# A long convolution and its soft mixture of experts on one core: first stage in three products, second-stage transfers in pairs, z loads in two blocks

One core of one Trainium2 chip. The metric is the device time of one execution in microseconds (us), the median of several runs. A ratio always compares fast runs of the same rounds on the same chip.

## The reference

```python
# x (8, 5696, 128), h (5696, 128); all float32
Xf = np.fft.rfft(x, n=2*S, axis=1); Hf = np.fft.rfft(h, n=2*S, axis=0)
y  = np.fft.irfft(Xf * Hf[None], n=2*S, axis=1)[:, :S, :]     # causal long convolution
x  = y.reshape(B * S, D)                                      # 45568 tokens
logits = x @ phi                                              # 8 experts x 4 slots
d = softmax over tokens;  slot_input = d.T @ x
slot_out[e] = max(slot_input[e] @ w1[e], 0) @ w2[e]
out = softmax over slots (logits) @ slot_out
```

## The kernel before

The transform of length 90 x 64 is done with matrix products, in three stages that a loop of steps runs side by side. A step `t` takes four columns and the four mirrored ones of one group (`h`, then the eight batches; eight steps a group).

- **First stage** (`stage_a`): load a piece of x, form sums and differences of mirrored columns on GpSimd (`fold`), two 128x128 products for the sums and two for the differences, evict on ScalarE, write to the array `f` in HBM.
- **Second stage** (`stage_b1`, `stage_b2`): for each unit (two frequencies; 23 a group, three a step) load `g` from `f`, product, multiply by the transform of h on VectorE, product back, evict, write to `z` in HBM.
- **Third stage** (`stage_c1` and on): once for two steps (a pair), load 90 rows of `z`, products, then logits and the running softmax.

All transfers of the loop are issued by SyncE, in program order.

```python
# first stage, once for the sums (comp 0), once for the differences (comp 1)
for G in range(2):
    p = bank()
    nc.tensor.matmul(p[:, :], s1[:, tab[G], :], src, start=True, stop=True)        # L204
    nc.scalar.activation(st[:, :, G, :], p, AF.Copy)                               # L206
for a, p in enumerate((F0, F1)):                       # two writes of 45 rows, 1 KB runs
    nc.sync.dma_start(out=fd[g][a, n0:n0 + CH] ..., in_=st[p:p + NP] ...)          # L210
# ... cut ...
t_ = bpool.tile([P, 2, 2, D], F32, name="gt", tag="gt", bufs=5)   # one unit, 256 KB
nc.sync.dma_start(out=t_ ..., in_=fd[g] ...)                                       # L223
# ... cut: in the loop, AHEAD = 4 ...
u = us.pop(0); prefetch(u + AHEAD); stage_b1(u)        # g is asked for four units ahead
# ... cut ...
st = bpool.tile([P, 2, 2 * D], F32, name="zst", tag="zst", bufs=3)
nc.scalar.activation(st, bz, AF.Copy); nc.sync.dma_start(out=zd[g - 1] ..., in_=st)  # L281, L282
# ... cut ...
zring = [ypool.tile([P, 2, CH, 2, D], F32, name=f"zc{i}") for i in range(2)]
# load_z: 90 rows of 8 KB to partitions 20..109; two of them a pair                  # L307
```

The tile framework adds the waits.

Of the kernel before, what the change touches and what calls it, by code (L numbers as in the profile page):

```python
# [10 lines left out]
F32 = mybir.dt.float32  # L11
# [5 lines left out]

def transform_tables(S, N1, N2, CH, Z0, X0, F0, F1):












    N, R1, HALF, P = N1 * N2, S // N2, N2 // 2, 2 * N2
    k1 = np.arange(N1)
    alpha = np.pi * (k1 + 0.5) / N1
    m1 = np.arange(R1) - (N1 - 1) / 2
    a1 = np.outer(m1, alpha)
    s1 = np.stack([np.cos(a1), -np.sin(a1), -np.cos(a1)], 1)
    a0 = np.outer(alpha, np.arange(N1 // 2) + 0.5)
    i1 = np.stack([np.cos(a0), -np.sin(a0), -np.cos(a0)], 1)
    NP = N1 // 2
    part = s1  # L40
    s1 = np.zeros((P, 3, P))
    for a, p in enumerate((F0, F1)):
        s1[X0:X0 + R1, :, p:p + NP] = part[:, :, a * NP:(a + 1) * NP]
    i1 = np.pad(i1[np.arange(N1).reshape(2, N1 // 2).T.reshape(-1)],
                [(Z0, P - N1 - Z0), (0, 0), (0, N2 - N1 // 2)])
    k2 = np.arange(N2)
    omega = np.pi * (k1[:, None] + 2 * N1 * k2[None] + 0.5) / N
    m2 = np.arange(HALF) - (N2 - 1) / 2
    a2 = m2[None, :, None] * omega[:, None, :]
    w = np.concatenate([np.cos(a2), np.sin(a2)], 1)  # L50
    back = np.arange(N2).reshape(2, HALF // CH, CH).transpose(1, 0, 2).reshape(-1)
    NU = (NP + 1) // 2
    turn = (N1 - 1) / 2 * alpha[:, None] + (N2 - 1) / 2 * omega
    wq = np.zeros((2, N2, NP, N2))
    vq = np.zeros((2, N2, NU, 2, N2))
    tn = np.zeros((2, N2, 2, NU, 2))
    for a in range(2):
        wq[a] = w[a * NP:(a + 1) * NP].transpose(1, 0, 2)
        for q in range(NP):
            vq[q % 2, :, q // 2, a] = w[a * NP + q][back].T  # L60
            tn[q % 2, :, 0, q // 2, a] = np.cos(turn[a * NP + q]) / N
            tn[q % 2, :, 1, q // 2, a] = np.sin(turn[a * NP + q]) / N
    wq, vq, tn = [t.reshape(P, *t.shape[2:]) for t in (wq, vq, tn)]
    return [np.ascontiguousarray(t, dtype=np.float32) for t in (s1, i1, wq, vq, tn)]
# [3 lines left out]
def kernel(  # L68
# [42 lines left out]
    SPLIT = R1 // 16 * 16  # L111
    Z0, X0, F0, F1 = 20, 20, 6, 82
    ctx.enter_context(tc.manual_schedule())

    t_s1, t_i1, t_w, t_v, t_turn = [
        nc.inline_tensor(t, f"tab_{n}").ap()
        for n, t in zip(("s1", "i1", "w", "v", "turn"), transform_tables(S, N1, N2, CH, Z0, X0, F0, F1))]
    fd = [nc.dram_tensor(f"f_{g}", (2, N2, NP, 2, D), F32, kind="Internal").ap() for g in range(B + 1)]
# [33 lines left out]

    s1 = apool.tile([P, 3, P], F32, name="s1", tag="s1", bufs=1)
    wt = fconst.tile([P, NP, HP], F32, name="wt")
# [10 lines left out]
    xs = {}  # L165
    xf = [apool.tile([P, CH, D], F32, name=f"x{i}", tag=f"x{i}", bufs=1) for i in range(2)]
    xcs = [apool.tile([P, 2, CH, D], F32, name=f"xc{i}", tag=f"xc{i}", bufs=1) for i in range(3)]
# [20 lines left out]
    def fold(c, comp):  # L188
        if c not in xs:
            return  # L190
        t_ = xs.pop(c) if comp else xs[c]
        y_ = xf[comp]
        nc.gpsimd.tensor_tensor(out=y_[:, :, :], in0=t_[:, 0, :, :], in1=t_[:, 1, ::-1, :],  # L193
                                op=AL.subtract if comp else AL.add)
        folded[(c, comp)] = y_

    def stage_a(c, comp):
        g, j = divmod(c, NJ)
        src = folded.pop((c, comp))
        tab = (0, 1) if comp == 0 else (1, 2)  # L200
        st = apool.tile([P, CH, 2, D], F32, name="fst", tag="fst", bufs=3)
        for G in range(2):
            p = bank()
            nc.tensor.matmul(p[:, :], s1[:, tab[G], :],  # L204
                             src[:, :, :].rearrange("p n d -> p (n d)"), start=True, stop=True)
            nc.scalar.activation(st[:, :, G, :],  # L206
                                 p[:, :].rearrange("p (n d) -> p n d", d=D), AF.Copy)
        n0 = comp * HALF + CH * j
        for a, p in enumerate((F0, F1)):
            nc.sync.dma_start(  # L210
                out=fd[g][a, n0:n0 + CH, :, :, :].rearrange("n q c d -> q n (c d)"),
                in_=st[p:p + NP, :, :, :].rearrange("k n c d -> k n (c d)"))


    gs, prods = {}, {}

    def load_g(u):
        if u >= (B + 1) * NU:
            return
        g, i = divmod(u, NU)  # L220
        n = min(2, NP - 2 * i)
        t_ = bpool.tile([P, 2, 2, D], F32, name="gt", tag="gt", bufs=5)
        nc.sync.dma_start(  # L223
            out=t_[:, 0:n, :, :].rearrange("p q c d -> p (q c d)"),
            in_=fd[g].rearrange("a r q c d -> (a r) (q c d)")[:, 4 * i * D:(4 * i + 2 * n) * D])
        gs[u] = t_

# [39 lines left out]
    def stage_b2(u):  # L267
# [6 lines left out]
        for q in range(n):  # L274
            r = slice(q * HP, (q + 1) * HP)
            for a in range(2):
                nc.tensor.matmul(bz[a * HP:(a + 1) * HP, q, 0:2 * D], vt[r, i, a, :],  # L277
                                 y_[r, a, :, :].rearrange("p c d -> p (c d)"),
                                 start=True, stop=True)
        st = bpool.tile([P, 2, 2 * D], F32, name="zst", tag="zst", bufs=3)  # L280
        nc.scalar.activation(st[:, 0:n, :], bz[:, 0:n, 0:2 * D], AF.Copy)  # L281
        nc.sync.dma_start(  # L282
            out=zd[g - 1][2 * i:2 * i + n, :, :, :].rearrange("q r c d -> r q (c d)"),
            in_=st[:, 0:n, :])

# [3 lines left out]
    ybufs = [ypool.tile([P, Q * CH, D + 1], F32, name=f"y{i}") for i in range(2)]  # L289
    zring = [ypool.tile([P, 2, CH, 2, D], F32, name=f"zc{i}") for i in range(2)]  # L290
    lt = ypool.tile([P, CH, 2, HP], F32, name="lt")
    dt = ypool.tile([P, CH, 2, HP], F32, name="dt")
    om, op = [ypool.tile([P, CH, D], F32, name=n) for n in ("om", "op")]
    yt = ypool.tile([D, Q * CH, 2, MH], F32, name="yt")
    for t_ in zring:
        nc.vector.memset(t_[:, :, :, :, :], 0.0)
    for t_ in (lt, dt):
# [3 lines left out]

    def load_z(c):
        b, j = divmod(c, NJ)
        t_ = zring.pop(0)
        zring.append(t_)
        w_ = 2 * CH * 2 * D
        nc.sync.dma_start(  # L307
            out=t_[Z0:Z0 + N1, :, :, :, :].rearrange("k o n c d -> k (o n c d)"),
            in_=zd[b].rearrange("q (a r) c d -> (q a) (r c d)",
                                a=2)[:, j * w_:(j + 1) * w_])  # L310
        zs[c] = t_

    def load_pair(T):
        if T < NT:
            load_z(2 * T)
            load_z(2 * T + 1)

    def stage_c1(T, between):
        za, zb = zs.pop(2 * T), zs.pop(2 * T + 1)
        y_ = ybufs[T % 2]  # L320
# [5 lines left out]
        def product(o, tab, q):  # L326
            p = bank()
            for h_, t_ in enumerate((za, zb)):
                nc.tensor.matmul(p[h_ * HP:(h_ + 1) * HP, :], i1[:, tab, :], t_[:, o, :, q, :],  # L329
                                 start=True, stop=True)  # L330
            return p[:, :].rearrange("p (n d) -> p n d", d=D)
# [197 lines left out]
    last_front = queue[-1][1] + 1  # L529
    AHEAD = 4  # L530
    loaded = 0

    load_x(0)
    nc.scalar.dma_start(out=s1[:, :, :], in_=t_s1)
    for c in range(1, 3):
# [9 lines left out]
    for t in range(steps):  # L545
# [6 lines left out]
        def prefetch(last):  # L552
            nonlocal loaded
            while loaded < len(queue) and queue[loaded][0] <= last \
                    and queue[loaded][0] // NU * NJ + NJ <= t:
                load_g(queue[loaded][0])
                loaded += 1

        def slot_b():
            fresh = bool(us)  # L560
            if fresh:
                u = us.pop(0)
                prefetch(u + AHEAD)
                stage_b1(u)
                wait_b2.append(u)
# [11 lines left out]
        if t < NA:  # L577
            load_x(t + 3)
            stage_a(t, 0)
            fold(t + 1, 0)  # L580
        if pair(3) is not None:
            dispatch(pair(3))
# [17 lines left out]
        if t < NA:  # L600
            stage_a(t, 1)
            fold(t + 1, 1)
        if pair(1) is not None:
# [8 lines left out]
        if t == NJ:  # L612
            prefetch(AHEAD)
        if t == NA:
# [5 lines left out]
        if t == last_front:  # L620
# [6 lines left out]
            w2s = last.tile([P, E, NFC, D], F32, name="w2s")  # L627
            for i in range(2):
                t_ = last.tile([P, 2, CH, 2, D], F32, name=f"zd{i}")
                nc.vector.memset(t_[:, :, :, :, :], 0.0)  # L630
                zring.insert(i, t_)
            assert pair(1) is not None
# [12 lines left out]
        if 0 <= i < E // 2:  # L645
            nc.sync.dma_start(
                out=w2s[:, 2 * i:2 * i + 2, :, :],
                in_=moe_w2[2 * i:2 * i + 2].rearrange("e (p c) d -> p e c d", p=P))
    assert list(Ls) == [NT - 1] and not (ys or ds or prods or gs or zs or xs or folded or wait_b2
                or kept or landed)  # L650
# [131 lines left out]
```

## Time and profile before

| | kernel before |
|---|---|
| median of 4 runs | 988.72 us (983.49 to 992.83) |
| profiled span | 980.8 us |
| steps 27 to 71 (all three stages at work) | 11.75 us each, alternately 10.64 and 12.87 |
| transfers issued a step | 13.2 |

"Step" times come from the starts of the first-stage products in the timeline. In a chain of waits each share is time in which the end of the program hung on that line; "X <- Y" in a wait table means that X stood still until Y.

### The profile page before, as it was taken

The numbers are of one execution on the slowest core, as the hardware profiler recorded it, in microseconds if no ns is written. First come the engines' busy times: TensorE is split into PE (matmuls) and PEld (weight loads), VectorE is DVE, ScalarE is ACT, GpSimd is POOL, SyncE is SP. The second block draws the span as 40 slices with busy tenths as digits, with TensorE's granted clock in tenths as the row PEclk, the third lists the DMA queues.
The fourth block names the chain that finished last, engine by engine and source line by source line (L and its number), as shares of the span: only waits on it lengthen the run. The fifth ranks groups of instructions, "written<-read, shape, count | busy, mean of one in ns | idle before, by whom it ended". The sixth has DMA issues, their size and how long they took to land.

```text
span 980.8 us, 20314 instructions
## 1 busy us (share of the span) xinstructions
PE 862.6 (88%) x7220; PEld 403.2 (41%) x7220; DVE 671.7 (68%) x1137; ACT 510.8 (52%) x1051; POOL 462.4 (47%) x427
## 2 busy tenths in 40 slices
PE   6778788899999999999999999999998887875893
PEld 2222233334444444444444444444443333332883
DVE  2034577568888878777878787777788996554542
ACT  3557545445666655556555565555554443443442
POOL 5546532245555555555555555555533432694000
PEclk9979999999999999999999999999999997797875
DMA  7988899899999998998999899989998996853598
GB/s 193 269 260 266 266 324 327 270 312 295 301 294 313 296 299 276 287 303 261 307 289 297 266 298 287 300 261 288 306 279 264 297 285 190 247 174 122 224 406 328
DMA packets 177283, 272.79 MB, mean 278 GB/s; under 512 B 15024, under 2 KB 119728, under 8 KB 171423
## 3 DMA queue, kind: packets, MB, share of 16 engines
q1 hardware_dynamic: 176607, 271.13, 88.7%
q8 instruction: 58, 0.95, 0.4%
q10 hardware_dynamic: 576, 0.36, 0.2%
q14 instruction: 42, 0.34, 0.1%
HBM read 143.04 MB, written 128.39 MB: 277 GB/s over the span
## 4 chain that ended last, share of the span: by engine, by line
PE 55%; DMA 22%; POOL 7%; DVE 6%; issue 3%; ACT 3%; SPq 2%; DVEq 0%; ACTq 0%; POOLq 0%
PE bank L204 19%; PE bank L329 11%; PE bt L237 9%; DMA z<-zst 8%; PE bz L277 6%; DMA zc<-z 5%; POOL y L348 5%; DMA out_dram<-o 4%; DMA gt<-f 3%; PE bank L357 3%; PE bank L442 2%; PE bank L366 2%; PE bank L395 1%; DVE yf L263 1%; DMA f<-fst 1%
## 5 line engine op out<-in xcount | busy, mean ns | idle before, releaser
L204 PE MATMUL bank<-x,s 128*128 128x512 f32 x576 | 287.3, 626 | 9.5 <-POOL x L193 7.9
L193 POOL TENSOR_TENSOR x<-xc 128x512 f32<-128x512 f32 x144 | 183.4, 1275 | 141.0 <-PE bank L204 124.6
L281 ACT ACTIVATE zst<-bz 128x512 f32<-128x512 f32 (+1 forms) x184 | 108.3, 588 | 222.6 <-PE bz L277 138.5
L206 ACT ACTIVATE fst<-bank 128x512 f32<-128x512 f32 x288 | 168.6, 597 | 86.0 <-PE bank L204 69.0
L258 DVE TENSOR_TENSOR pr<-bt,Hr 128x512 f32<-128x512 f32 (+1 forms) x184 | 126.6, 688 | 81.3 <-PE bt L237 77.2
L237 PE MATMUL bt<-gt,wt 64*64 64x256 f32 x1620 | 138.2, 404 | 37.6 <-PE bz L277 9.9
L263 DVE TENSOR_TENSOR yf<-pr,pi 128x512 f32<-128x512 f32 (+1 forms) x184 | 158.1, 859 | 6.4
L204 PEld LDWEIGHTS bank<-x,s 128*128 128x128 f32 x576 | 100.5, 193 | 132.8 <-issue 89.0
L329 PE MATMUL bank<-zc,i 128*64 128x512 f32 x480 | 137.6, 620 | 17.3 <-ACT y L338 11.4
L261 DVE TENSOR_TENSOR pi<-bt,Hi 128x512 f32<-128x512 f32 (+1 forms) x184 | 125.2, 681 | 0.0
L277 PE MATMUL bz<-yf,vt 64*64 64x256 f32 x1440 | 118.1, 382 | 7.0 <-DVE yf L263 4.5
L237 PEld LDWEIGHTS bt<-gt,wt 64*64 64x64 f32 x1620 | 44.4, 132 | 154.7 <-PE bank L204 52.4
L348 POOL TENSOR_TENSOR y<-y,op 128x512 f32<-128x512 f32 x64 | 75.7, 1183 | 59.2 <-DVE op L334 56.6
L348 POOL TENSOR_TENSOR y<-y,om 128x512 f32<-128x512 f32 x64 | 85.4, 1334 | 2.5
L403 POOL MEMSET dt<- 64x8 f32 x32 | 3.4, 107 | 175.8 <-ACT dn L406 115.3
L277 PEld LDWEIGHTS bz<-yf,vt 64*64 64x64 f32 x1440 | 53.4, 132 | 45.0 <-issue 9.5
L357 PE MATMUL bank<-ident,y 109*128 109x109 f32 x512 | 60.7, 266 | 10.5 <-POOL y L348 10.4
L329 PEld LDWEIGHTS bank<-zc,i 128*64 128x64 f32 x480 | 32.5, 138 | 87.3 <-issue 40.5
L359 ACT ACTIVATE yt<-bank 128x360 f32<-128x360 f32 x128 | 53.0, 471 | 29.3 <-PE bank L357 29.2
L248 DVE SCALAR_TENSOR_TENSOR Hr<-bt,turn,ph 128x128 f32<-128x128 f32 (+1 forms) x46 | 16.0, 349 | 76.0 <-ACT ph L246 76.0
L357 PEld LDWEIGHTS bank<-ident,y 109*128 109x128 f32 x512 | 49.6, 143 | 26.4 <-POOL y L348 17.0
L334 DVE TENSOR_TENSOR y<-bank,y 128x512 f32<-128x512 f32 x32 | 22.1, 690 | 44.9 <-ACT y L338 36.8
(95 smaller groups left out, 911.1 us busy)
## 6 DMA issues: line engine op xcount, KB each, us to landing
f<-fst SPq DMA_DIRECT2D x288, 180.0 KB
gt<-f SPq DMA_DIRECT2D x198, 256.0 KB
z<-zst SPq DMA_DIRECT2D x176, 256.0 KB
zc<-z SPq DMA_DIRECT2D x60, 720.0 KB
xc<-in_x_dram SPq DMA_DIRECT2D x64, 320.0 KB
out_dram<-o SPq DMA_DIRECT2D x16, 1024.0 KB
out_dram<-o SPq DMA_DIRECT2D x8, 768.0 KB
c_t<-cst SPq DMA_DIRECT2D x26, 180.0 KB
```

The source lines that it names most:

```text
L193: nc.gpsimd.tensor_tensor(out=y_[:, :, :], in0=t_[:, 0, :, :], in1=t_[:, 1, ::-1, :], op=AL.subtract if comp else AL.add)
L204: nc.tensor.matmul(p[:, :], s1[:, tab[G], :], src[:, :, :].rearrange("p n d -> p (n d)"), start=True, stop=True)
L206: nc.scalar.activation(st[:, :, G, :], p[:, :].rearrange("p (n d) -> p n d", d=D), AF.Copy)
L237: nc.tensor.matmul(bt[q * HP:(q + 1) * HP, a, 0:2 * D], wt[r, 2 * i + q, :], t_[r, q, :, :].rearrange("p c d -> p (c d)"), start=True, sto ...
L258: nc.vector.tensor_tensor(out=pr[r, :, :, :], in0=pv, in1=Hr[r, i, :, :].unsqueeze(2).broadcast_to([n * HP, 2, 2, D]), op=AL.mult)
L261: nc.vector.tensor_tensor(out=pi[r, :, :, :], in0=pv, in1=Hi[r, i, :, :, :], op=AL.mult)
L263: nc.vector.tensor_tensor(out=y_[r, :, :, :], in0=pr[r, :, :, :], in1=pi[r, :, ::-1, :], op=AL.add)
L277: nc.tensor.matmul(bz[a * HP:(a + 1) * HP, q, 0:2 * D], vt[r, i, a, :], y_[r, a, :, :].rearrange("p c d -> p (c d)"), start=True, stop=True)
L281: nc.scalar.activation(st[:, 0:n, :], bz[:, 0:n, 0:2 * D], AF.Copy)
L329: nc.tensor.matmul(p[h_ * HP:(h_ + 1) * HP, :], i1[:, tab, :], t_[:, o, :, q, :], start=True, stop=True)
L348: nc.gpsimd.tensor_tensor(out=part_, in0=part(v, 0), in1=o_[:, :, :], op=sign)
L357: nc.tensor.transpose(p[:, i * TR:(i + 1) * TR], ys[T][0:TR, k * CH + i, 0:D], ident[0:TR, 0:TR])
```

## The change

The intent: (1) the four first-stage products have 90 useful columns of 128; side by side in column halves the same work fits into three. (2) Fewer, longer transfers in the second stage. (3) z loads of 16 KB runs, in a block of 64 rows and one of 26, so that the engines meet the ports of the on-chip memory evenly.

```diff
-        for G in range(2):
-            nc.tensor.matmul(p[:, :], s1[:, tab[G], :], src ...)
+        n = 1 if late else 2                     # two products early in the step, one late
+        for G in range(n):
+            for h_ in range(2):                  # sums in columns 0..63, differences in 64..127
+                nc.tensor.matmul(p[h_ * HP:(h_ + 1) * HP, :], s1[:, h_, 2 * late + G, :],
+                                 folded[(c, h_)] ...)
-        for a, p in enumerate((F0, F1)):         # 2 writes, twice a step
+        # early: for each half 45 + 15 rows in 1 KB runs; late: 60 rows in 512 B runs: 6 writes a step
-        t_ = bpool.tile([P, 2, 2, D], F32, name="gt", tag="gt", bufs=5)
+        t_ = bpool.tile([P, 4, 2, D], F32, name="gt", tag="gt", bufs=2)      # two units, 512 KB
-                prefetch(u + AHEAD)
+                prefetch(u + 2 - u % NU % 2)
-        st = bpool.tile([P, 2, 2 * D], F32, name="zst", tag="zst", bufs=3)
+        if i % 2 == 0:
+            zst.append(bpool.tile([P, 4, 2 * D], F32, name="zst", tag="zst", bufs=2))
+        # ... evict into its half; one write for two units
-    zring = [ypool.tile([P, 2, CH, 2, D], F32, name=f"zc{i}") for i in range(2)]
+    zring = [ypool.tile([P, 2, 2, CH, 2, D], F32, name="zc")]
+        for r, n, p in [(0, 64, 32), (64, 26, 0)]:    # rows, count, first partition; 16 KB runs
+            nc.sync.dma_start(out=t_[p:p + n] ..., in_=zd[b] ...[r:r + n, ...])
     # cut: both folds of the next step at once, into a second pair of tiles; tables; a zero-filled tile
```

## The prediction

> **What bounds the kernel now.** I read the page first (busy shares, the slices, the chain), then the windows by stage, then the groups with shapes, the timeline of one step, and last the records of the single DMA packets.
>
> ```profile
> PE 862.6 (88%) x7220; PEld 403.2 (41%) x7220; DVE 671.7 (68%) x1137; ACT 510.8 (52%) x1051; POOL 462.4 (47%) x427
> ...
> PE 55%; DMA 22%; POOL 7%; DVE 6%; issue 3%; ACT 3%; SPq 2%; DVEq 0%; ACTq 0%; POOLq 0%
> PE bank L204 19%; PE bank L329 11%; PE bt L237 9%; DMA z<-zst 8%; PE bz L277 6%; DMA zc<-z 5%; POOL y L348 5%; DMA out_dram<-o 4%; DMA gt<-f 3%; PE bank L357 3%; PE bank L442 2%; PE bank L366 2%; PE bank L395 1%; DVE yf L263 1%; DMA f<-fst 1%
> ```
>
> TensorE carries 55% of the chain and its largest piece is the first stage (L204, 19%); but the chain keeps crossing over to transfers of the intermediate arrays (z 8 and 5%, gt 3%). The windows (columns: stretch, length, busy us of each engine with counts, granted clock, mean share of the 16 DMA engines, GB/s) say why:
>
> ```profile
> 140.00:300.00 160.00, 149.24 (x1174) 63.95 (x1172) 119.99 (x188) 86.06 (x161) 72.79 (x62) 0.99 0.97 303
> 300.00:500.00 200.00, 194.58 (x1603) 86.22 (x1600) 159.41 (x256) 113.83 (x224) 106.28 (x92) 1.00 0.96 289
> ...
> 930.00:981.00 51.00, 32.68 (x431) 29.69 (x427) 19.29 (x32) 16.30 (x32) 0.00 (x0) 0.60 0.95 366
> ```
>
> From 140 to 700 us both TensorE (97%) and the DMA engines (96%) are full. And the DMA engines are full at 289 GB/s, while the output stage gets 366 out of the same share: there the bytes are cheap, here they are dear. The packet records give the medians 46 ns for 1 KB, 84 for 2 KB, 159 for 4 KB (a line: 8.5 ns + 37.6 per KB), but 511 for the 8 KB packets of the z loads, where the line and their own minimum say 309. One pair's z load (180 packets) takes 6.3 to 6.8 us even when little else moves.
>
> A step is one pass of the main loop. By the starts of the first-stage products in the timeline, steps 0 to 8 take 3.5 to 4.2 us, 10 to 17 about 7.6, 18 to 24 8.3, and the 44 steps from 202.5 to 719.6 us 11.75 on average: every second one a steady 10.65 (TensorE without a gap), the other 11.2 to 14.4, in which the z loads and z writes are waited for. The best pairs take 21.6 us, the average 23.5; so TensorE alone would give some 10.8 a step, and waits on transfers add the rest.
>
> ```profile
> L204 PE MATMUL bank<-x,s 128*128 128x512 f32 x576 | 287.3, 626 | 9.5 <-POOL x L193 7.9 <-ACT fst L206 1.5
> L206 ACT ACTIVATE fst<-bank 128x512 f32<-128x512 f32 x288 | 168.6, 597 | 86.0 <-PE bank L204 69.0 <-DMA f<-fst 14.4 <-DMA z<-zst 1.5
> L281 ACT ACTIVATE zst<-bz 128x512 f32<-128x512 f32 x176 | 105.2, 598 | 219.8 <-PE bz L277 135.9 <-DMA z<-zst 72.9 <-PE bank L329 6.4
> ```
>
> To be seen here: a product instruction lists 626 ns, its eviction 597; the first stage hardly waits for its own operands (9.5 us); and ScalarE waited 72.9 us for a z staging buffer to be written out, the plainest sign in the profile that writes fall behind.
>
> **What the Trainium skill says.** "TensorEngine Tiling (Array Packing)", Theoretical Speedup: column tiles of at most 64 outputs give up to 2x. The trace agrees for the third stage, which already works so: eight 128x64 instructions of 512 columns take 1.87 to 1.93 us (L329), as long as four 128x128 ones (L204, 1.91 to 1.98). "DMA: Bandwidth & Descriptors", Why a DMA increments its semaphore by 16: the transfer uses the largest count up to 16 that divides the slowest dimension on both sides. So 45 and 90 rows run on 15 engines, 64 rows on 16, 26 on 13. No view of the kernel before shows single engines, so this is taken on trust. "SBUF — State Buffer", Door 1: a transfer's partitions decide which of 16 ports it uses. 64 rows from partition 32 cover all 16, 4 rows each; 90 rows from 20, six to an engine, collide. That would explain 511 against 309 ns; the full-width 2 KB output writes sit at 85, on the line. Same DMA page, Specifications: line rate from 512 B up; the kernel before has no 512 B packets, its 768 B ones took 36 ns, on the line.
>
> **The change part by part.**
> (1) First stage. Of four full products a step (two for sums, two for differences) three remain, each made of sum and difference side by side in column halves. One product is two instructions of 0.43 us (the cadence in the timeline), so TensorE loses 0.86 us a step, 72 x 0.86 = 62 us in all; column halves should cost nothing extra. ScalarE loses one eviction a step, 72 x 0.597 = 43 us, off the path. Both folds of the next step now go into a second buffer pair, so GpSimd no longer waits for TensorE (124.6 us in the wait table), also mostly off the path.
> (2) First-stage writes. Before, 4 x 180 = 720 packets of 1 KB a step, 48 on each of 15 engines: 48 x 46 ns = 2.21 us. After: 480 of 1 KB and 480 of 512 B (the late product has one component per partition), 32 x 46 + 32 x 27 (line) = 2.34 us. A small loss.
> (3) Second stage. g loads 4 KB a row instead of 2: 12 x 159 instead of 24 x 84 ns, about 0.1 us a step saved. z writes keep their 1 KB packets, only half as many issues. The buffer lead shrinks: g has two tiles of two units, asked for 2 units ahead instead of 4; z staging keeps about 3 slots.
> (4) z loads. Before 12 packets of about 510 ns an engine and pair, 6.1 us. After, if ports are the reason: the 64 rows 4 x 610 = 2.4 us on all engines, the 26 rows 2 packets, at two engines a port some 2.2 us on 13 engines: 4.7 us a pair, so 0.7 us a step less on the busiest engines.
>
> Sum for a full step. TensorE: 10.8 - 0.86 = 9.9 us. DMA, busiest engines, with the stretched means (1 KB 50, 2 KB 105 ns): before f 2.4, x 1.3, g 2.4, z writes 2.2, z loads 3.05, c 0.25 = 11.6, which agrees with the 11.75 seen: this is why I call DMA the co-bound. After: 2.6 + 1.3 + 2.0 + 2.2 + 2.35 + 0.25 = 10.7; with every packet on the line 9.8. VectorE has 159.4/200 x 11.75 = 9.4 us. So TensorE's gain can be used only as far as DMA gives way: I take 10.65 a step, 44 x 1.1 = 48 us. Steps 18 to 24: TensorE 8.3 to 7.4, DMA 8.3 to some 7.9: 3 us. Steps 9 to 17: 3 us. Steps 0 to 8: TensorE 3.5 to 2.6, but DMA has 2.34 + 1.0 or more, so nothing. After 720 us there is no first stage; shorter z loads, 2 us. Together 56 us: 991.5 - 56 = 936.
>
> **The rivals.**
> (A) The z loads stay slow (the 64 KB distance of rows in memory rather than ports is the reason): then DMA stays near 11.5 a step and only some 15 to 20 us come: about 973. For it: 511 ns also when the load is nearly alone; against: that is what a collision inside one load would show too.
> (B) A new wait: g two units ahead is about 7 us, and the chain shows g and z landings of 9 to 11 us. If 1 us a step is lost so, 44 us go back: about 975. Against: the before kernel waited for g only in a few places (10 us in all), and shorter z loads shorten the queue ahead of g.
> (C) 512 B writes cost as much as 1 KB ones: 32 x 19 ns = 0.6 us a step back, about 960.
> (D) DMA gives way fully: the pair falls to TensorE's 19.8 us, 22 x 3.7 = 81 us and some 10 elsewhere: about 903.
>
> **Range and chances.** A, B and C are each perhaps one in six and rarely all at once; D one in eight. Hence 936 with 906 to 968. Over 2% faster (below 971.6): 0.87; within 2%: 0.10; slower: 0.03, which needs B and C together.
>
> **What would show it.** Right: first-stage matmul instructions 864 with half-array shape, first-stage busy TensorE share down, full steps near 10.6 us, TensorE still over 90% and the DMA share still over 0.93 in 300 to 500; a z load under 5.5 us; GB/s per share above 300; ScalarE's wait for z writes below 73 us. Wrong: steps at 11.5 with z packets of 1 us (A); waits of TensorE for gt in tens of us (B); 512 B packets over 40 ns (C); TensorE at 97% and DMA below 0.9 (D).

## The result

The changed kernel takes 1125.38 us (median of 4, 1120.64 to 1132.55); the ratio to the kernel before is 1.139, 95% interval 1.130 to 1.148. Ratios here and below are the mean time of one kernel's fast runs over that of the other's in the same rounds, so not quite the ratio of medians. It is 14% slower, not 5% faster.

The chain of waits after (the page, part 4):

```profile
PE 52%; DMA 32%; DVE 4%; issue 3%; POOL 3%; SPq 2%; ACT 1%; DVEq 0%; POOLq 0%; ACTq 0%
DMA gt<-f 22%; PE bank L216 15%; PE bt L259 11%; PE bank L351 10%; PE bz L299 6%; DMA zc<-z 5%; DMA out_dram<-o 3%; PE bank L379 3%; POOL y L370 2%; PE bank L464 2%; SPq L232 2%; PE bank L417 2%; DVE pr L280 1%; PE bank L440 1%; DVE pi L283 1%
```

The loads of g went from 3% of the chain to 22%, some 246 us of 1125. The windows by stage, with the columns as before:

```profile
140.00:300.00 160.00, 118.82 (x922) 41.92 (x924) 93.65 (x141) 58.36 (x103) 48.93 (x40) 0.87 0.83 252
300.00:500.00 200.00, 166.83 (x1486) 70.36 (x1484) 140.90 (x225) 94.61 (x185) 99.70 (x84) 0.91 0.83 251
```

TensorE fell from 97% to 83% busy, its granted clock from 1.00 to 0.91, and the transfer engines from 96% to 83%. None of them is full any more: that points to a latency rather than to a lack of throughput. The group of the second stage's first product names it:

```profile
L259 PE MATMUL bt<-gt,wt 64*64 64x256 f32 x1620 | 155.6, 453 | 189.9 <-DMA gt<-f 168.0
L216 PE MATMUL bank<-x,s 128*64 128x512 f32 x864 | 261.7, 707 | 12.0 <-POOL x L205 11.6
```

TensorE stood 168.0 us before this product for g; before the change it was 9.5 (total us, times, longest):

```profile
PE bt L237 <- DMA gt<-f: 9.5, 3, 7.9
```

One such wait in the timeline (start, length, engine, line, operation; SPq is SyncE issuing):

```profile
443.09 0.67 SPq L244 DMA_DIRECT2D gt<-f  x1
...
447.40 0.34 SPq L499 DMA_DIRECT2D c_t<-cst  x1
448.10 0.83 SPq L227 DMA_DIRECT2D f<-fst  x2
449.03 0.57 SPq L244 DMA_DIRECT2D gt<-f  x1
450.69 0.33 PEld L259 LDWEIGHTS bt<-gt,wt 64*64 64x64 f32 x8 [6.84 <-issue]
450.72 0.71 PE L259 MATMUL bt<-gt,wt 64*64 64x256 f32 x4 [6.21 <-DMA gt<-f]
```

The load issued at 443.09 is the one that TensorE needs next; TensorE starts on it 7.6 us later and stands still for 6.2 us of that. Its tile had been free since 432.9 us: SyncE, which works in program order, came to this load only after four first-stage writes, at 442.99. This suggested the first theory, **LEAD**: g is asked for two units ahead, and two units of work are shorter than a landing. But the TensorE time saved had to show as well, once g is no longer late.

### The profile page after: what moved, and what is told of

Its sections match the earlier page's. It is cut to its first block, busy times and chain, and to the rows that moved or that the text cites. A ratio compares the mean times of both kernels' runs of the same rounds, so it can differ in the third digit from the quotient of the medians.

```text
span 1125.1 us, 20498 instructions
## 1 busy us (share of the span) xinstructions
PE 870.7 (77%) x7508; PEld 381.4 (34%) x7508; DVE 675.6 (60%) x1135; ACT 477.0 (42%) x979; POOL 469.4 (42%) x427
## 4 chain that ended last, share of the span: by engine, by line
PE 52%; DMA 32%; DVE 4%; issue 3%; POOL 3%; SPq 2%; ACT 1%; DVEq 0%; POOLq 0%; ACTq 0%
DMA gt<-f 22%; PE bank L216 15%; PE bt L259 11%; PE bank L351 10%; PE bz L299 6%; DMA zc<-z 5%; DMA out_dram<-o 3%; PE bank L379 3%; POOL y L370 2%; PE bank L464 2%; SPq L232 2%; PE bank L417 2%; DVE pr L280 1%; PE bank L440 1%; DVE pi L283 1%
## 5 line engine op out<-in xcount | busy, mean ns | idle before, releaser
L259 PE MATMUL bt<-gt,wt 64*64 64x256 f32 x1620 | 155.6, 453 | 189.9 <-DMA gt<-f 168.0
L216 PE MATMUL bank<-x,s 128*64 128x512 f32 x864 | 261.7, 707 | 12.0 <-POOL x L205 11.6
L205 POOL TENSOR_TENSOR x<-xc 128x512 f32<-128x512 f32 x144 | 199.5, 1412 | 93.9 <-PE bank L216 76.4
L219 ACT ACTIVATE fst<-bank 128x512 f32<-128x512 f32 x216 | 126.9, 597 | 114.7 <-PE bank L216 92.7
L285 DVE TENSOR_TENSOR yf<-pr,pi 128x512 f32<-128x512 f32 (+1 forms) x184 | 167.6, 911 | 6.4
L299 PE MATMUL bz<-yf,vt 64*64 64x256 f32 x1440 | 134.3, 427 | 6.9 <-DVE yf L285 6.3
L351 PE MATMUL bank<-zc,i 128*64 128x512 f32 x480 | 127.2, 655 | 3.2 <-DMA zc<-z 3.2
L283 DVE TENSOR_TENSOR pi<-bt,Hi 128x512 f32<-128x512 f32 (+1 forms) x184 | 125.2, 680 | 0.0
L216 PEld LDWEIGHTS bank<-x,s 128*64 128x64 f32 x864 | 63.5, 156 | 141.2 <-issue 107.0
L299 PEld LDWEIGHTS bz<-yf,vt 64*64 64x64 f32 x1440 | 60.8, 148 | 53.5 <-issue 14.0
L752 PE MATMUL op<-so,cT 32*128 32x128 f32 x704 | 46.4, 375 | 4.2 <-ACT o L761 3.6
```

The lines of the kernel that those rows point to most:

```text
L205: nc.gpsimd.tensor_tensor(out=y_[:, :, :], in0=t_[:, 0, :, :], in1=t_[:, 1, ::-1, :], op=AL.subtract if comp else AL.add)
L216: nc.tensor.matmul(p[h_ * HP:(h_ + 1) * HP, :], s1[:, h_, 2 * late + G, :], folded[(c, h_)][:, :, :].rearrange("p n d -> p (n d)"), start= ...
L219: nc.scalar.activation(st[:, :, G, :], p[:, :].rearrange("p (n d) -> p n d", d=D), AF.Copy)
L259: nc.tensor.matmul(bt[q * HP:(q + 1) * HP, a, 0:2 * D], wt[r, 2 * i + q, :], t_[r, q, :, :].rearrange("p c d -> p (c d)"), start=True, sto ...
L283: nc.vector.tensor_tensor(out=pi[r, :, :, :], in0=pv, in1=Hi[r, i, :, :, :], op=AL.mult)
L285: nc.vector.tensor_tensor(out=y_[r, :, :, :], in0=pr[r, :, :, :], in1=pi[r, :, ::-1, :], op=AL.add)
```

## The experiments

Eighteen kernels ran. "Issues" is the number of transfers that SyncE issues a step in steps 27 to 71, "step" their mean length, both from the profiled run; each ratio is to the kernel before.

| run | what it is | issues | step us | ratio (95%) |
|---|---|---|---|---|
| before | | 13.2 | 11.75 | 1 |
| after | the change | 12.3 | 13.46 | 1.139 (1.130 to 1.148) |
| e1 | change, g as before: singles, 4 ahead | 13.8 | 12.03 | 1.004 (0.999 to 1.009) |
| e8 | change, g singles, 2 ahead | 13.7 | 13.48 | 1.140 (1.135 to 1.145) |
| e2 | change, g pairs, 4 ahead; z writes single | 13.8 | 11.59 | 0.987 (0.983 to 0.990) |
| e7 | first stage and z loads only | 15.2 | 11.91 | 1.013 (1.007 to 1.019) |
| e3 | first stage only | 15.2 | 12.36 | 1.027 (1.021 to 1.033) |
| e5 | z loads only | 13.2 | 11.55 | 0.979 (0.973 to 0.985) |
| e4 | g pairs 4 ahead only | 11.75 | 11.56 | 0.987 (0.982 to 0.992) |
| e6 | z writes in pairs only | 11.75 | 11.51 | 0.979 (0.973 to 0.985) |
| e9 | e3, late product in 1 KB runs (wrong result) | 15.2 | 12.41 | 1.023 (1.016 to 1.031) |
| e11 | before, four writes cut into six | 15.2 | 12.45 | 1.032 (1.025 to 1.039) |
| e14 | e3, z loads issued by ScalarE | 14.25 + 1 | 12.73 | 1.034 (1.026 to 1.042) |
| e12 | e4, e5 and e6 together | 10.4 | 11.07 | 0.961 (0.954 to 0.968) |
| e15 | change, g pairs 4 ahead | 12.4 | 11.37 | 0.967 (0.956 to 0.979) |
| e17 | e15, late writes issued by ScalarE | 10.5 + 2 | 13.31 | 1.088 (1.080 to 1.096) |
| e18 | e11, two of six issued by ScalarE | 13.2 + 2 | 13.53 | 1.099 (1.091 to 1.108) |
| e19 | e12, two of four writes issued by ScalarE | 8.4 + 2 | 12.92 | 1.055 (1.047 to 1.064) |
| e21 | e15, x in one load | 11.6 | 10.98 | 0.958 (0.952 to 0.964) |
| e20 | e12, x in one load | 9.6 | 11.07 | 0.958 (0.952 to 0.963) |

### The lead of g

e1 puts g back to single units:

```diff
-        t_ = bpool.tile([P, 4, 2, D], F32, name="gt", tag="gt", bufs=2)
+        t_ = bpool.tile([P, 2, 2, D], F32, name="gt", tag="gt", bufs=5)
-                prefetch(u + 2 - u % NU % 2)
+                prefetch(u + AHEAD)              # AHEAD = 4
```

> The changed kernel with the g loads alone put back: one unit (256 KB) a transfer, five tiles, asked for four units ahead. Theory LEAD (the 137 us lost come from asking for g only two units ahead): about 930 to 950 us, TensorE's wait for gt falls from 168 us to under 20. Theory SIZE (512 KB in one piece lands later and holds up the rest): the same here, this run does not part the two. Rival ELSEWHERE (the first stage in column halves, its 512 B writes or the new z loads cost the time, and gt is only where it shows): stays above 1080 us.

e8 is e1 with `bufs=3` and `AHEAD = 2`: the old size, the new lead.

> As the first run of this call (g loads of one unit), but with three tiles and asked for only two units ahead, the changed kernel's lead with the old transfer size. LEAD: slow again, 1080 to 1130 us. SIZE: fast, 930 to 960 us. A result half way (1000 to 1060) would say that both have a share.

e2 keeps the pairs and gives them the old lead (z writes single for the room):

```diff
-        t_ = bpool.tile([P, 4, 2, D], F32, name="gt", tag="gt", bufs=2)
+        t_ = bpool.tile([P, 4, 2, D], F32, name="gt", tag="gt", bufs=3)
-                prefetch(u + 2 - u % NU % 2)
+                prefetch(u + 4 - u % NU % 2)
```

> The changed kernel with its 512 KB g loads kept, but three tiles instead of two and asked for four units ahead; for the room, the z writes are one unit each again (three tiles). LEAD: 930 to 955 us. SIZE: above 1050 us. ELSEWHERE: above 1080 us.

e7 is e1 with the z writes single as well.

> The changed kernel with both of the second stage's transfers put back to one unit, g four ahead: what is left is the first stage in three products and the z loads. LEAD and SIZE: within 1% of the run that puts back the g loads alone, 930 to 950 us; if the pairing of the z writes had a cost of its own, this one is faster by that. ELSEWHERE: above 1080 us.

Measured: e8 1132.73, e1 998.94, e2 979.80, e7 1008.72 us. LEAD is right about the loss and SIZE falls: small transfers with a lead of two are as slow as the change, and with a lead of four large ones are faster than small ones (e2 against e7, which differ in g alone). TensorE's wait for g, from the wait tables of e8 and of e2 (total us, times, longest):

```profile
PE bt L259 <- DMA gt<-f: 177.2, 45, 10.6
```

```profile
PE bt L259 <- DMA gt<-f: 23.4, 9, 11.7
```

But e1, e2 and e7 all missed the 930 to 955 us that LEAD expected with its gain (and e8 lies 3 us above its range). The lead explains why the change lost 14%; it does not explain why, mended, it gains next to nothing. ELSEWHERE was wrong about the size of its effect and right that there is one. Which loads of g come late, and why, is told below with the semaphores.

### Each part alone

> The kernel before with the first stage of the change alone (three products, six writes a step). Theory DMA BOUND (in the full steps the transfer engines are the limit already, so that TensorE's 62 us turn into waits): 985 to 1010 us, full steps 11.6 us or more, TensorE under 90% from 300 to 500 us, waits for z loads and z writes up. Theory TENSORE BOUND (the prediction): 940 to 955 us.

> The kernel before with the new z loads alone. PORTS (the z load gets cheaper and the others keep their price, as predicted, 0.35 us less of all engines' time a step): 970 to 985 us, 2 KB packets stay at 106 ns mean. SHARED LIMIT (what one kind of load gains in packet time the others lose, the total stays near 302 GB/s of busy time): 985 to 998 us, with the 2 KB packets dearer, 115 ns or more.

> The kernel before with g loads of two units in three tiles, asked for four units ahead; z writes, first stage and z loads as before. If half as many, longer g packets are worth something by themselves: 965 to 980 us (the pair with and without this in the first call differ by 2.6%). If they only pay where the new z loads are: 985 to 998 us.

> The kernel before with the z writes in pairs alone (two tiles of two units). Same packets of 1 KB, half the issues: within 1% of before, 983 to 997 us. Slower by more than 1% would say that the staging became the wait, with ScalarE's wait for z writes well above 73 us.

Measured: e3 1022.21, e5 975.25, e4 982.16, e6 974.85 us. This turned the prediction on its head. The part that was to carry the gain, three products for four, makes the kernel 2.7% slower by itself; the part that was to be nothing, z writes in pairs with the very same packets, is worth 2.1%. My expectation for e6 (within 1%) missed, and e4 fell between its two ranges (965 to 980, 985 to 998). e5 lies in the range of PORTS, though its 2 KB packets went from 106 to 110 ns. For e3 both ranges missed: it is 12 us slower than even DMA BOUND allowed, TensorE was busy for 91% of the window of 300 to 500 us (under 90 was expected), and the transfer engines' share there was 0.94 against 0.96 before, so "the engines are full" does not fit as the reason.

What e3 adds and e6 takes away is the number of transfers: 15.2 and 11.75 a step against 13.2. Two readings were possible: many short packets (the 512 B writes), or many issues.

> Wrong result on purpose. The kernel before with the first stage of the change alone (1.027 of before), but the late product is written as 1 KB runs from 30 partitions instead of 512 B runs from 60: the same six issues and the same bytes, 720 packets a step instead of 960. Theory PACKETS (the many short packets cost the 2.7%): 0.98 to 1.00 of before. Theory ISSUE (SyncE, which issues the transfers one by one and in order, falls behind, so that the z load of the next pair is asked for later): stays at 1.015 to 1.03.

> The kernel before, correct, with its four first-stage writes a step cut into six (45, 15 and 30 rows for each half) of the same 1 KB packets and the same bytes; nothing else touched. ISSUE: slower than before by 1.5 to 3%, z loads issued a microsecond or more later after the start of their step (3.3 us in the kernel before). PACKETS: within 0.7% of before.

e11 touches nothing but this:

```diff
-        for a, p in enumerate((F0, F1)):
+        for a, q0, q1, p in ((0, 0, NP, F0), (1, 0, 15, F1), (1, 15, NP, F1)):
             nc.sync.dma_start(
-                out=fd[g][a, n0:n0 + CH, :, :, :].rearrange("n q c d -> q n (c d)"),
-                in_=st[p:p + NP, :, :, :].rearrange("k n c d -> k n (c d)"))
+                out=dst[a, :, q0:q1, :, :].rearrange("n q c d -> q n (c d)"),
+                in_=st[p + q0:p + q1, :, :, :].rearrange("k n c d -> k n (c d)"))
```

Same bytes, same packets, same products, two issues more a step: 1.032, as slow as e3. Its chain of waits shows where the time hangs, on z loads (5% in the kernel before):

```profile
PE 44%; DMA 35%; POOL 5%; SPq 4%; ACT 4%; DVE 4%; issue 3%; ACTq 0%; DVEq 0%; POOLq 0%
DMA zc<-z 18%; PE bank L204 13%; PE bank L330 10%; DMA z<-zst 7%; PE bt L238 7%; PE bz L278 5%; DMA out_dram<-o 4%; POOL y L349 3%; DMA gt<-f 3%; SPq L211 2%; PE bank L443 2%; PE bank L358 2%; DMA f<-fst 1%; PE bank L419 1%; ACT fst L206 1%
```

The transfer engines' share from 300 to 500 us fell to 0.93, so they do not look like its limit. e9, with 720 packets of 1 KB for 960 mixed ones, stays at 1.023, within the interval of e3 (1.027). PACKETS falls: the packet records of e3 give the 512 B packets a median of 27 ns and a mean of 31, what the prediction took for them. The number of transfers costs, about 1.6% for each one a step in e11.

### Why a transfer costs time by being one more

My first reading, ISSUE, was that SyncE needs its own time for each issue and so asks for z later: from the start of the step to the z load's issue it is (mean) 3.3 us before, 4.6 in e3, 4.8 in e11, but 2.5 in e6 and in e4. So I moved issues to ScalarE.

> The kernel before with the first stage of the change alone, but the z loads issued by ScalarE (its own queue) instead of SyncE. ISSUE: the z load no longer waits behind SyncE's other issues, so that the first stage's gain shows: 940 to 985 us. Transfer engines as the only limit (DMA BOUND): 1005 to 1025 us, as with SyncE (1022).

> The kernel before with its four first-stage writes cut into six (1.032 when SyncE issues all), two of the six issued by ScalarE. SYNCE: 0.99 to 1.01 of before. ENGINES: 1.02 to 1.04.

> As the run before it, with the two late writes a step issued by ScalarE right after its own eviction, so that SyncE has 10.5 issues a step. SYNCE (the cost is in its in-order issuing): 0.92 to 0.955 of before, z loads issued within 1 us of their step's start. ENGINES (the cost is in the transfers themselves, whoever issues them): within 1% of the run before it.

> The version without the new first stage (0.961), with two of its four first-stage writes a step issued by ScalarE. TensorE already carries 69% of its chain and z loads are issued 0.9 us after their step's start, so SyncE is no longer what it waits for: 0.955 to 0.967 of before under both theories.

Here `nc.sync.dma_start` becomes `nc.scalar.dma_start` for the transfers named. None brought the gain: 1.034, 1.099, 1.088, 1.055. e14, where the z loads moved, is within the noise of e3 (1.027), 3 us above the range of DMA BOUND; there the z loads' share of the chain fell from 20% to 2% and the time stayed. In e18, e17 and e19, where first-stage writes moved, the same transfers cost more than under either theory. The wait table of SyncE's queue in e18 shows what happens: its writes of z (L283) and loads of g (L224) wait for first-stage writes.

```profile
SPq L283 <- DMA f<-fst: 87.7, 33, 5.5
...
SPq L224 <- DMA f<-fst: 69.3, 27, 7.1
SPq L224 <- DMA zc<-z: 59.7, 17, 4.9
SPq L211 <- DMA f<-fst: 55.5, 33, 4.1
```

This led to the last theory, **WINDOW**: eight completion semaphores (counters that tell of a transfer's landing), handed out in turn, mean that a transfer waits until the one eight before it, in the program's order, has landed, whoever issued either; at most eight are in flight. The timeline of the kernel before shows it at a z load:

```profile
414.69 1.57 SPq L307 DMA_DIRECT2D zc<-z  x2
417.06 1.20 SPq L182 DMA_DIRECT2D xc<-in_x_dram  x2
418.37 0.81 SPq L210 DMA_DIRECT2D f<-fst  x2
419.27 0.38 SPq L223 DMA_DIRECT2D gt<-f  x1
419.75 0.39 SPq L282 DMA_DIRECT2D z<-zst  x1
422.54 0.33 SPq L477 DMA_DIRECT2D c_t<-cst  x1
...
426.22 1.08 PE L329 MATMUL bank<-zc,i 128*64 128x512 f32 x4 [0.27 <-DMA zc<-z]
426.25 0.32 SPq L223 DMA_DIRECT2D gt<-f  x1
```

Count from the second z load: x, x, f, f, g, z, c are seven. The eighth, a load of g, goes out at 426.25, just when the z load has landed and TensorE starts on it (426.22); for 3.4 us before that SyncE issues nothing. For all 22 z loads of steps 27 to 71 in the sixteen kernels whose loop issues from SyncE alone, the eighth transfer after the second z part was never issued earlier than 0.43 us after the last z packet; the medians are 0.8 to 1.0 us. The second part of a z load lands 7.5 us (change) to 10.4 us (e9) after its issue (medians), so for that long only seven other transfers can go out, and more transfers for the same work mean that less of the work gets through. In e11 seven are spent with fewer bytes; in e6 and e4 they go further.

The semaphore records of the packed traces settle that this rule held: in all twenty traces, 19,369 times a transfer followed another on the same semaphore, and never was it issued before the earlier one had been counted in full. They also say how SyncE spent a step (us, steps 27 to 71; "semaphore" is waiting for the transfer's own semaphore, "other" any other wait, for data or a free buffer; about 1 us a step between instructions is left out):

| run | step | issuing | semaphore | other |
|---|---|---|---|---|
| before | 11.75 | 6.7 | 2.7 | 1.1 |
| e11 | 12.45 | 7.8 | 2.9 | 0.35 |
| e6 | 11.51 | 5.8 | 2.3 | 2.3 |
| e12 | 11.07 | 5.9 | 0.6 | 3.7 |
| e18 | 13.53 | 6.2 | 6.0 | 0.1 |
| after | 13.46 | 6.3 | 1.9 | 4.3 |

In the kernel before, 2.25 of the 2.7 us were spent behind z loads; in e18, 3.7 of the 6.0 behind writes of the other queue. So e18 does not refute SYNCE, as I first took it to: it freed 1.6 us of issuing and lost 3.1 to the semaphores. What the table shows is that in e11 SyncE has hardly a pause left: two more issues took 1.1 us more of issuing (0.51 us each, on average) and 0.2 us more of semaphore waits, where 0.8 us of slack was to be had. Issuing time and window fill SyncE together; what each is worth alone would take a kernel with more semaphores, and none was run.

The same records tell which loads of g come late in the changed kernel. Of the 66 in its steps 27 to 71, 44 were issued 8.4 us or more (median 9.2) before TensorE was ready for them, landed after 4.6 (median), and stopped it for less than 1 us each. The other 22, one for each pair of z transfers, had 0.3 to 3.9 us (median 2.5), landed after 6.3, and stopped TensorE for 95 us, 2.2 us a step. Of these, 21 used a semaphore that a z transfer had held, and 18 were kept back by it. In e15, with a lead of four, 16 loads were kept back in the same way, but none of these had less than 6.9 us, and no load stopped TensorE for over 1 us. The loss of the change is thus the short lead meeting the window, and not every load.

Two last runs took an issue away without taking bytes:

```diff
-        for r in (slice(0, SPLIT), slice(SPLIT, R1)):           # 80 + 9 rows
+        for r in ((slice(0, 96),) if 0 < g < B else (slice(0, SPLIT), slice(SPLIT, R1))):
```

> The whole change with g asked for four units ahead (0.967 of before, 12.4 issues a step), and x loaded for seven of the nine groups as 96 rows in one transfer instead of 80 + 9 in two: one issue a step less, 8% more x bytes; the surplus rows meet zeros in the table, the result is correct. WINDOW (at most eight transfers in flight, so that the number of transfers decides): 0.94 to 0.96 of before. TRAFFIC (packets and bytes decide): 0.967 to 0.98.

> The version without the new first stage (0.961, 10.4 issues a step) with the same one-transfer x load, 9.4 issues a step. TensorE is 69% of its chain already, so WINDOW gives little: 0.95 to 0.961. TRAFFIC: 0.961 to 0.97. If both hold as expected by WINDOW, the new first stage is worth something only here at the end: the two runs within 1.5% of each other.

Measured 954.64 and 955.49 us: 0.958 and 0.958, both in the ranges of WINDOW. e21's gain over e15 (0.967, another call) is inside the two intervals' overlap, so by itself it is only a sign; its step of 10.98 us against 11.37 in the profiled runs points the same way. Both intervals (0.952 to 0.964, 0.952 to 0.963) speak against TRAFFIC, e21's clearly (0.967 to 0.98), e20's not by itself (0.961 to 0.97). One issue fewer also saves SyncE issuing time, so these two runs do not part that from the window.

### What combines

> A version that may beat both: the kernel before with the new z loads, the z writes in pairs and g loads in pairs four units ahead (three tiles), without the new first stage. If the single gains (2.1, 2.1 and 1.3%) add up: 0.945 of before, 938 to 950 us. If they all ease the same thing: 0.97 to 0.98, 965 to 978 us.

> The whole change, its z writes in pairs too, with one thing mended: g has three tiles of two units and is asked for four units ahead (for the room the late product has one staging tile instead of two). 12.5 issues a step against 13.2 in the kernel before and 10.4 in the version without the new first stage (0.961). If the number of issues decides: between these two, 0.965 to 0.985 of before. If the first stage's 62 us come through once nothing else is short: 0.91 to 0.94.

e12 (955.91 us) leaves the first stage as it was; e15 (971.14 us, in the range of "the number of issues decides") is the whole change with three g tiles and a lead of four:

```diff
-        t_ = bpool.tile([P, 4, 2, D], F32, name="gt", tag="gt", bufs=2)
+        t_ = bpool.tile([P, 4, 2, D], F32, name="gt", tag="gt", bufs=3)
-                prefetch(u + 2 - u % NU % 2)
+                prefetch(u + 4 - u % NU % 2)
-        st = apool.tile([P, CH, n, D], F32, name="fst", tag=f"fst{n}")
+        st = apool.tile([P, CH, n, D], F32, name="fst", tag=f"fst{n}", bufs=n)
```

e12's three gains of 2.1, 2.1 and 1.3% come to 3.9% together, between adding up and easing the same thing; both expected ranges missed. Its chain of waits and its window of 300 to 500 us show why it ends there:

```profile
PE 69%; DMA 11%; DVE 7%; POOL 6%; issue 3%; ACT 2%; SPq 1%; DVEq 0%; ACTq 0%; POOLq 0%
```

```profile
300.00:500.00 200.00, 200.00 (x1732) 92.80 (x1730) 169.16 (x275) 123.63 (x243) 114.79 (x100) 1.00 0.97 310
```

TensorE is busy in all of the 200 us. The same window of e21, the best version with the new first stage:

```profile
300.00:500.00 200.00, 193.97 (x1824) 81.42 (x1816) 176.87 (x279) 115.49 (x229) 120.34 (x103) 0.99 1.01 316
```

Here the transfer engines are full (a mean share of 1.01, overlapping packets counted twice) and TensorE is at 97%. e20 and e21 end at the same time with different limits; that the engines are e21's is not shown, since SyncE too has only 0.75 us a step left there. Both, and e12, beat the kernel before by 4% and the change by about 16% (0.958 / 1.139 = 0.84, from different calls). e12 is the simplest of the three.

## Why the prediction was wrong, step by step

- **"The buffer lead shrinks: g has two tiles of two units, asked for 2 units ahead instead of 4."** The step was seen and left out of the sum; rival B gave it a sixth and 1 us a step of the full ones, 44 us. The mechanism was named, the size was the failure: between the change and e15, which differ in the g tiles, the lead and one staging tile, a full step goes from 11.37 to 13.46 us, and steps 10 to 24, where I allowed no loss, take 155 us instead of 120; in all 154 us (1125 to 971, two calls). The lead of about 7 us and the landings of 9 to 11 us were taken for every load alike, and set aside because the kernel before waited little for g. The runs show unlike loads: two in three had 9.2 us and landed in 4.6, while the one behind each z load, mostly held back by it, had 2.5 us left and landed in 6.3, and that alone is 2.2 us a step, as much as the whole difference of the full steps (2.1). The kernel before held such loads back too (15 of them in steps 27 to 71), but with four units of lead none had under 8.3 us.
- **"A small loss" for the first-stage writes, "only half as many issues" for the z writes.** Transfers were priced by packets alone. The term that was missing is the number of transfers: two more a step cost 3.2% (e11), 1.4 fewer gave 2.1% (e6). In e3 it eats the whole first-stage gain: 62 us of TensorE work less by the prediction's count, and 2.7% more time. SyncE, which has to issue them all, is not in the prediction's sum.
- **"TensorE's gain can be used only as far as DMA gives way": 11.6 to 10.7 us a step.** Where the lead is mended (e2) the packets of a step still take 11.4 us of the engines' time. z loads fell from 2.86 to 2.51 us of all engines' mean and f writes stayed near 2.3, but g packets of 4 KB averaged 223 ns, not the 167 ns that my 2.0 us implied, and the rate in busy time stayed at 302 GB/s against 303. Why the loads stretch is open; the rate was 292 in e3 and 295 in e11 (15.2 issues a step), 301 to 307 from 15.2 issues (e7) down to 11.75 (e6), and 313, 319 and 321 in e21, e12 and e20 with fewer.
- **(1) TensorE, 0.86 us a step.** Right in the count: 864 instructions of half-array shape. But in every second step, the one without a z load, 10.64 became 10.14 (e15) to 10.36 us (e9), 0.3 to 0.5 of the 0.86 us. What takes the other half is not settled; the chain of e15 has 7% for GpSimd and 6% for VectorE, and GpSimd, which was to wait no longer for TensorE, still does for 55.0 us (124.6 before).
- **(4) z loads by ports.** Right: alone 2.1%, 21 us; sorted by length, the shorter 64 of a load's 90 packets take 654 to 713 ns on average (608 at best), the longer 26 take 1204 to 1319, near twice 608, as two engines a port would have it. (The records do not name a packet's rows, so the sorting stands in for them.) e5 also shortened the waits for z's semaphores, so that SyncE's semaphore waits fell from 2.7 to 2.0 us a step; the two ways of gaining are not parted. The rival that the distance of rows in memory slows them (A) falls.
- **Rival C** (512 B packets at 46 ns) falls: 27 ns median, and e9 changes nothing.
- **Rival D** (a pair of steps at TensorE's 19.8 us) did not come: the best pair of e15 took 20.4 us, the average 22.7. In e12 the pair is at TensorE's limit, but without the new first stage.

## What to carry to other kernels

Halving the buffers to double the transfers keeps the bytes and halves the lead: compare the time that the consumer takes for what is still in the other buffer with the landing time, and do it for the load that is issued behind the longest transfer, not for the average one; that one set the loss here. Where a long load is in flight, count transfers as well as bytes and packets; a work-saving change that needs more transfers can lose by them, and moving writes to a second engine made it worse here, where both shared the semaphores. Test each part of a bundled change alone: here the part meant to win lost, and the one meant to be neutral won.

## What the Trainium skill lacked or had wrong

- "DMA: Bandwidth & Descriptors" (Why a DMA increments its semaphore by 16 and not by 1) asks for one semaphore for each transfer in flight, but has nothing on what it costs when a program hands out a few in turn and issues in order. With eight in turn: in none of 19,369 cases was a transfer issued before the earlier one on its semaphore had landed, and SyncE stood 2.7 us of a step of 11.75 for that.
- The same page (Issuing engines are not separate DMA queues) says that issuing from several engines only saves the sequencer's time, "which is usually small relative to the DMA itself". One issue is small here too (0.51 us on average, where a g load lands in 4.6); what the page lacks is that 13 of them fill 6.7 us of a step of 11.75, and that the saving can become a loss where the engines share semaphores: 1.032 became 1.099 when ScalarE issued two of six writes (e18), and 0.961 became 1.055 (e19).
- The same page's rule to issue early and wait late, and the SBUF page's to coalesce, have no number for the lead that coalescing costs: two units instead of four, 1.140 against 1.004 at equal transfer size (e8, e1).
- Not lacking: "SBUF — State Buffer", Door 1, agreed. The z load of 64 rows over all 16 ports and 26 rows on 7 had 64 packets of 16 KB near the best (654 to 713 ns on average, 608 at best) and 26 at about twice that.
